# Attention followed by a mixture of experts: the order of vector work around seven-product matrix multiplications, scalar work in program order, and the last stores on two queues

## The chip, the cores and the metric

The kernel runs on one core of one Trainium2 chip. The metric is the device time of one execution in microseconds (us). Engines are named as in the profile: PE multiplies matrices (PEld is its weight load), DVE is the vector engine, ACT the scalar engine, POOL is GpSimd, SP only issues transfers. PE leaves its results in *banks* of a memory called PSUM, where DVE and ACT read them.

## The reference

Attention of 4 batches, 8 heads, 768 positions and head size 64 gives x of 3072 tokens by 512. Routing weights P come from x by eight rounds of row and column normalization. Then each of 8 experts is applied to every token:

```python
for e in range(E):                       # 8 experts
    h = np.maximum(x @ w1[e], 0.0)       # 3072 x 1024
    ye = h @ w2[e]                       # 3072 x 512
    out += P[:, e:e + 1] * ye
```

## The kernel before

Expert 0 is computed inside the attention stage. Experts 1 to 7 run in 42 *steps*, one for each expert e and chunk c of 512 tokens. Both layers of a step use seven half-size products in place of eight (the Strassen scheme), on sums and differences that DVE makes beforehand: S of the left factor, T of the right. Layer 1 does its seven products twice, for two halves g of the hidden units. A pair (g, k) below is product k of half g. Layer 2 of a step runs interleaved with layer 1 of the following step, in seven slots:

```python
        def step(g, k):
            ...                                    # cut
            if k == 6:
                product(g, 6, "y"); copy("2", "y")       # ACT: R copy of PSUM bank y
            if k == 7:
                product(g, 7, "y"); relu_sum(g, 1, 1, "y", "5")   # DVE reads bank y
            if k == 3:
                product(g, 3, "w", last=True); relu_sum(g, 0, 1, "w", "2")
            if k == 4:
                product(g, 4, "y", last=True)            # PE adds into bank y again
                nc.scalar.activation(out=block(g, 1, 0), in_=banks["y"], func=AF.Relu, ...)
        for pair in (((0, 1), (0, 2)), ((0, 6), (0, 5)), ((0, 7), (0, 3)), ((0, 4), (1, 1)),
                     ((1, 6), (1, 5)), ((1, 7), (1, 2)), ((1, 3), (1, 4))):
            for g, k in pair: step(g, k)
            yield
```

```python
    with tc.manual_schedule(engines={mybir.EngineType.DVE}):     # DVE runs in program order
        ...                                                      # cut
            if e == 1:
                weight_first(c)               # ACT: acc *= P[:, 0], all four blocks at once
                xg = combine_x((c + 1) % NCH)
            for slot in range(7):
                run(l1g, 1); run(l2g, 1)      # (shortened)
                if slot == 0: run(hg, 1)      # S of layer 2: second of four
                if slot == 1: run(hg, 2)      # third and fourth
                if slot in (3, 4):
                    run(wg, 1)                # weight combination for the next expert
                    run(xg, 2)                # T of x, only in the first expert
            hg = combine_h(e, c); run(hg, 1)  # first of four S
```

Only DVE runs in program order. A scheduler orders PE and ACT when the program is built, from its own estimates. Layer 2's products are added into acc with their routing weight: four of seven by DVE, three by ACT into an `add` buffer and from there by an accumulating transfer. In the last step DVE does all seven. The stores of the last expert go out through SP.

A reader of the timelines needs a few names. `acc` is the running sum of the output. `R` is ACT's copy of a bank whose sum isn't finished; a *relu sum* of DVE adds such a copy to a bank and cuts off below 0. `l1y<-T,w` is product 4 of layer 1, alone in having T and w as inputs. `hT<-l1y` on DVE is the relu sum of product 7, which reads the same bank. `S<-hT` is a combination for layer 2, `S<-w` (or `T<-w`) one for the next expert's weights.

The softmax here doesn't subtract the row's maximum and nothing guards it: scores larger than these inputs give would overflow.

Of the kernel before, what the change touches and what calls it, by code (L numbers as in the profile page):

```python
# [10 lines left out]
F32 = mybir.dt.float32  # L11
F16 = mybir.dt.float16
U32 = mybir.dt.uint32
AF = mybir.ActivationFunctionType
# [25 lines left out]
def kernel(  # L40
# [13 lines left out]
    nc = tc.nc  # L54
# [3 lines left out]
    E = moe_w_gate.shape[1]  # L58
# [93 lines left out]
    def load_expert(e):  # L152
        return load_w1(e), load_w2(e)

    expw = {}
# [212 lines left out]
    def run(g, n):  # L368
        for _ in range(n):
            if next(g, "end") == "end":  # L370
                return False
        return True
# [164 lines left out]
    def weight_first(c):  # L537

        for nb in range(4 * c, 4 * c + 4):
            nc.scalar.activation(out=acc_of(nb), in_=acc_of(nb), func=AF.Copy,  # L540
                                 bias=0.0, scale=Pne[:, nb, 0:1])

    works = [(e, c) for e in range(1, E) for c in range(NCH)]
    lefts1, rights1, lefts2, rights2, hTs = {}, {}, {}, {}, {}
# [45 lines left out]
    def layer1_plain(e, c):  # L590
        new_h(e, c)
        w1 = expw[e][0]
        for fb in range(8):
            l1 = psB.tile([128, CH], F32, tag="l1", name="l1b")
            for dc in range(4):
                nc.tensor.matmul(
                    out=l1, lhsT=w1[:, dc, ts(fb, 128)], rhs=xT[dc // 2][:, dc % 2, ts(c, CH)],
                    start=(dc == 0), stop=(dc == 3),
                )
            nc.scalar.activation(out=hTs[e, c][:, :, fb, :],  # L600
                                 in_=l1.rearrange("p (q m) -> p q m", q=2), func=AF.Relu,
                                 bias=0.0, scale=1.0)
            yield

    def layer1(e, c):

        new_h(e, c)
        h = hTs[e, c]
        banks, R = {}, {}

        def product(g, k, bank, first=False, last=False):
            if first:
                banks[bank] = psB.tile([128, 2, 256], F32, tag="l1", name=f"l1{bank}")
            for f in range(2):
                for dc in range(2):
                    nc.tensor.matmul(  # L616
                        out=banks[bank][:, f, :],
                        lhsT=lefts1[e][k - 1][:, dc, ts(2 * g + f, 128)],
                        rhs=rights1[c][k - 1][:, dc, :], start=(first and f == 0 and dc == 0),
                        stop=(last and f == 1 and dc == 1), skip_group_check=True,  # L620
                    )

        def copy(name, bank):
            R[name] = mp.tile([128, 2, 256], F32, tag=f"R{name}", bufs=1, name=f"R{name}")
            nc.scalar.activation(out=R[name], in_=banks[bank], func=AF.Copy, bias=0.0, scale=1.0)  # L625

        def block(g, i, n):
            return h[:, n, 4 * i + 2 * g:4 * i + 2 * g + 2, :]

        def relu_sum(g, i, n, bank, name):  # L630
            nc.vector._custom_dve(TENSOR_ADD_SAT, out=block(g, i, n), in0=banks[bank],  # L631
                                  in1=R[name], s0=65504.0, s1=0.0)

        def step(g, k):
            if k == 1:
                product(g, 1, "y", first=True)
                copy("1", "y")
            if k == 2:
                product(g, 2, "z", first=True, last=True)
                relu_sum(g, 0, 0, "z", "1")  # L640
            if k == 6:
                product(g, 6, "y")
                copy("2", "y")
            if k == 5:
                product(g, 5, "w", first=True)
                copy("5", "w")
            if k == 7:
                product(g, 7, "y")
                relu_sum(g, 1, 1, "y", "5")
            if k == 3:  # L650
                product(g, 3, "w", last=True)
                relu_sum(g, 0, 1, "w", "2")
            if k == 4:
                product(g, 4, "y", last=True)
                nc.scalar.activation(out=block(g, 1, 0), in_=banks["y"], func=AF.Relu,  # L655
                                     bias=0.0, scale=1.0)

        for pair in (((0, 1), (0, 2)), ((0, 6), (0, 5)), ((0, 7), (0, 3)), ((0, 4), (1, 1)),
                     ((1, 6), (1, 5)), ((1, 7), (1, 2)), ((1, 3), (1, 4))):
            for g, k in pair:  # L660
                step(g, k)
            yield

    def store(c, i, n):
        for o in range(2):
            nc.sync.dma_start(
                out=out[ts(c, CH), :].rearrange("(q i p c) (n d) -> i n c p q d", q=2, i=2, c=2, n=2)[i, n, o],
                in_=acc[c][64 * o:64 * o + 64, i, n, :, :],
            )

    def layer2(e, c):
        banks = {}
        final = (e, c) == works[-1]

        def product(k, bank, first, last=False):
            if first:
                banks[bank] = psB.tile([128, 2, 256], F32, tag="l2", name=f"l2{bank}")
            for q in range(2):
                for f in range(4):
                    nc.tensor.matmul(  # L680
                        out=banks[bank][:, q, :], lhsT=lefts2[e, c][k - 1][:, q, f, :],
                        rhs=rights2[e][k - 1][:, f, :], start=(first and q == 0 and f == 0),
                        stop=(last and q == 1 and f == 3), skip_group_check=True,
                    )

        def add(bank, i, n, by_dma):
            if by_dma:
                t = mp.tile([128, 2, 256], F32, tag="add", bufs=3, name="add")
            for q in range(2):
                dst = acc[c][:, i, n, q, :]  # L690
                w = Pne[:, 4 * c + 2 * q + i, e:e + 1]
                if by_dma:
                    nc.scalar.activation(out=t[:, q, :], in_=banks[bank][:, q, :], func=AF.Copy,  # L693
                                         bias=0.0, scale=w)
                else:
                    nc.vector.scalar_tensor_tensor(  # L696
                        out=dst, in0=banks[bank][:, q, :], scalar=w, in1=dst,
                        op0=ALU.mult, op1=ALU.add,
                    )
            if by_dma:  # L700
                nc.gpsimd.dma_start(out=acc[c][:, i, n, :, :], in_=t, accum_op=ALU.add)  # L701


        steps = {
            1: ("y", True, False, (0, 0)), 2: ("z", True, True, (0, 0)), 5: ("w", True, False, (1, 1)),
            6: ("y", False, False, (0, 1)), 3: ("w", False, True, (0, 1)),
            7: ("y", False, False, (1, 1)), 4: ("y", False, True, (1, 0)),
        }
        done = {}
        for k in (1, 5, 6, 2, 7, 3, 4):  # L710
            bank, first, last, (i, n) = steps[k]
            product(k, bank, first, last)
            add(bank, i, n, k in (2, 3, 4) and not final)
            done[i, n] = done.get((i, n), 0) + 1
            if e == E - 1 and done[i, n] == (1 if (i, n) == (1, 0) else 2):
                store(c, i, n)
            yield



    with tc.manual_schedule(engines={mybir.EngineType.DVE}):
        l1g, l2g, hg, wg, xg = layer1_plain(*works[0]), iter(()), iter(()), iter(()), iter(())
        for n, (e, c) in enumerate(works):
            if c == 0 and e + 1 < E:
                expw[e + 1] = load_expert(e + 1)
            if c == 2 and e + 1 < E:
                wg = combine_w(e + 1)
            if e == 1:
                weight_first(c)
                xg = combine_x((c + 1) % NCH)  # L730
            for slot in range(7):
                run(l1g, 2 if n == 0 and slot == 0 else 1)
                run(l2g, 1)
                if slot == 0:
                    run(hg, 1)
                if slot == 1:
                    run(hg, 2)
                if n == 0:
                    if slot == 0:
                        run(combine_w(1), 9)  # L740
                if slot in (3, 4):
                    run(wg, 1)
                    run(xg, 2)
            hg = combine_h(e, c)
            run(hg, 1)
            l2g = layer2(e, c)
            if n + 1 < len(works):
                l1g = layer1(*works[n + 1])
        run(hg, 9)
        run(l2g, 9)  # L750


# [33 lines left out]
```

## Time and profile before

The kernel takes 745.61 us (median of 15 runs; 744.29 to 746.96). I split the profiled execution by instructions:

| stretch | from, to (us) | length |
|---|---|---|
| attention and routing | 0 to the first matmul of expert 1, 206.66 | 206.66 |
| expert 1, up to the seventh start of layer 2 | 206.66 to 292.08 | 85.41 |
| 34 steady steps | 292.08 to 717.36 | 425.28 |
| last step's layer 1 | 717.36 to 728.91 | 11.55 |
| tail: last layer 2, stores, end | 728.91 to 745.55 | 16.64 |

(The starts used are those of layer 2's first product, `l2y<-w,hT`.) The busy times on the page, and the window view for the steady stretch (window, its length, busy us and instructions of each engine, granted clock, DMA busy share, GB/s):

```profile
PE 718.8 (96%) x7078; PEld 582.5 (78%) x7078; DVE 564.7 (76%) x1115; ACT 426.7 (57%) x794; POOL 156.5 (21%) x190
...
292.08:717.36 425.28, 424.00 (x3811) 372.19 (x3808) 347.85 (x652) 229.19 (x477) 92.47 (x110) 1.00 0.56 94
```

PE looks full: 424.00 of 425.28 us. That is misleading, because a matmul's slice (0.27 us) is longer than the distance between two starts (0.109 us), so short holes are covered. The Trainium skill says so too ("Perfetto Trace Analysis", "Identifying the Most-Contended Engine": matmul busy time is no measure of the distance to the limit, the weight loads' share is better). Here weight loads fill 372.19/425.28 = 87.5%; one takes 97.7 ns on the mean, so dense issue would give 97.7/109.1 = 89.6%. The two holes are in the timeline (start, duration, engine, line, operation, tiles, shapes, count, and in brackets the idle time before with its releaser). A light step, which makes no weight combination:

```profile
508.62 0.68 DVE L553 TENSOR_TENSOR S<-hT 128x1024 f16<-128x1024 f16 x1
...
509.21 0.68 DVE L553 TENSOR_TENSOR S<-hT,S 128x1024 f16<-128x1024 f16 x1
...
509.81 0.71 PE L680 MATMUL l2z<-w,hT 128*128 128x256 f16 x5
509.82 0.68 DVE L631 CUSTOM_DVE_ANT_0 hT<-l1y,R 128x512 f16<-128x512 f32 x1
...
510.55 0.60 PE L616 MATMUL l1y<-T,w 128*128 128x256 f16 x4
510.55 0.31 PEld L616 LDWEIGHTS <-w 128*128 128x128 f16 x3 [0.21 <-issue]
```

Five l2z matmuls from 509.81 would let the next start at 510.36, but product 4 starts at 510.55. The profile calls the wait "issue", that is, it shows no cause; the neighbour on DVE does: the relu sum that reads the bank ends at 509.82 + 0.68 = 510.50. DVE did it late because two S, from 508.62 on, came first. A heavy step (four of six chunks) has a second hole, before product (1,4):

```profile
312.76 0.88 DVE L696 SCALAR_TENSOR_TENSOR acc<-l2y,Pne,acc 128x256 f32<-128x256 f32 x2 [0.78 <-PE l2y L680]
...
313.56 0.68 DVE L553 TENSOR_TENSOR S<-S,w 128x1024 f16<-128x1024 f16 x1
314.15 0.68 DVE L631 CUSTOM_DVE_ANT_0 hT<-l1y,R 128x512 f16<-128x512 f32 x1
314.31 0.60 PE L616 MATMUL l1w<-xT,S 128*128 128x256 f16 x4
...
314.89 0.60 PE L616 MATMUL l1y<-T,w 128*128 128x256 f16 x4
```

DVE idles 0.78 us for an accumulation's product and then does a weight combination ahead of the relu sum, which ends at 314.83. Product (1,4) could start at 314.75, 0.44 after `l1w`, and starts at 314.89. Light steps take 12.42 us and heavy ones 12.57, where 112 matmuls of 109.1 ns make 12.22.

In expert 1, ACT weights all of acc in a crowd (the source view: count, durations, first and last start):

```profile
L540 ACT ACTIVATE acc<-acc,Pne x24: 705/779/867, 208.7 to 233.5; 128x512 f32<-128x512 f32 x24
```

At the end, the timeline shows SP's last stores and DVE's last accumulation, the window view how busy the DMA engines are meanwhile:

```profile
729.60 12.35 SPq L666 DMA_DIRECT2D out_dram<-acc  x15
737.40 0.88 DVE L696 SCALAR_TENSOR_TENSOR acc<-l2y,Pne,acc 128x256 f32<-128x256 f32 x2 [0.34 <-PE l2y L680]
...
738.00:743.00 5.00, 0.00 (x0) 0.00 (x0) 0.28 (x1) 0.00 (x0) 0.00 (x0) 0.76 0.93 196
```

DVE is done at 738.28, yet the program ends at 745.55. In the trace the last ten stores leave SP 0.67 us apart, from 735.29 to 741.34.

### The profile page before, as it was taken

What the parts mean: (1) busy time and instruction counts of PE and PEld (TensorE: products, weight loads), DVE (VectorE), ACT (ScalarE), POOL (GpSimd) and SP (SyncE); (2) the same over time, 40 slices, a digit from 0 to 9 for tenths busy, and PEclk for the clock granted to TensorE, in tenths of its full rate; (3) what the DMA queues carried; (4) which work ended last, traced back from release to release, by engine and by line L of the source; (5) the groups of instructions that cost most, each with busy time, mean ns of one, the idle gap of its engine ahead of it and who ended that gap; (6) DMA issues with size and microseconds to landing.
All of it is one profiled execution on the core that took longest, in us unless ns stands there. A gap on an engine that the chain in (4) does not pass through costs nothing.

```text
span 745.6 us, 17358 instructions
## 1 busy us (share of the span) xinstructions
PE 718.8 (96%) x7078; PEld 582.5 (78%) x7078; DVE 564.7 (76%) x1115; ACT 426.7 (57%) x794; POOL 156.5 (21%) x190
## 2 busy tenths in 40 slices
PE   6999999999999999999999999999999999999994
PEld 2566666766668888888888888888888888888883
DVE  6557465664778998788778878887888788877775
ACT  2766677767488454545555555555555555555551
POOL 8313021000002122212221131213121312121210
PEclk8899999999999999999999999999999999999998
DMA  9999475200063339543954396438643864245877
GB/s 123 187 172 84 47 58 46 29 2 2 4 110 68 62 58 147 94 72 57 145 98 71 58 141 102 72 58 132 109 72 55 136 105 77 48 81 104 153 146 152
DMA packets 84656, 65.89 MB, mean 88 GB/s; under 512 B 50400, under 2 KB 64736, under 8 KB 84576
## 3 DMA queue, kind: packets, MB, share of 16 engines
q0 software_dynamic: 77520, 58.48, 55.2%
q1 hardware_dynamic: 7056, 6.30, 3.7%
q8 instruction: 55, 0.90, 0.5%
q14 instruction: 25, 0.20, 0.1%
HBM read 52.45 MB, written 6.29 MB: 79 GB/s over the span
## 4 chain that ended last, share of the span: by engine, by line
PE 64%; DVE 3%; issue 1%; ACT 0%; DVEq 0%; ACTq 0%
PE l1y L616 19%; PE l2y L680 18%; PE l2w L680 9%; PE l1w L616 9%; PE l1z L616 5%; PE l2z L680 4%; DVE S L553 1%; DVE acc L696 1%; DVE hT L631 1%; ACT R L625 0%; ACT hT L655 0%; ACT add L693 0%; DVEq L781 0%; ACTq L625 0%; ACTq L693 0%
## 5 line engine op out<-in xcount | busy, mean ns | idle before, releaser
L701 POOL DMA_DIRECT2D acc<-add x123 | 103.5, 841 | 402.6 <-ACT add L693 377.0
L625 ACT ACTIVATE R<-l1y 128x512 f32<-128x512 f32 x164 | 98.9, 603 | 126.6 <-PE l1y L616 91.7
L680 PEld LDWEIGHTS <-S 128*128 128x128 f16 x1344 | 131.5, 98 | 16.3 <-issue 1.1
L616 PEld LDWEIGHTS <-S 128*128 128x128 f16 x1312 | 128.3, 98 | 17.2 <-issue 1.9
L696 DVE SCALAR_TENSOR_TENSOR acc<-l2y,Pne,acc 128x256 f32<-128x256 f32 x254 | 110.3, 475 | 39.3 <-PE l2y L680 39.3
L616 PEld LDWEIGHTS <-w 128*128 128x128 f16 x984 | 95.8, 97 | 23.0 <-issue 12.0
L680 PEld LDWEIGHTS <-hT 128*128 128x128 f16 x1008 | 98.5, 98 | 12.7 <-issue 1.1
L429 ACT ACTIVATE PT<-sc 128x1024 f16<-128x1024 f32 (+1 forms) x96 | 84.2, 919 | 40.5 <-PE sc L420 38.3
L616 PE MATMUL l1y<-T,S 128*128 128x256 f16 x656 | 98.4, 272 | 0.9 <-ACT R L625 0.7
L680 PE MATMUL l2y<-T,S 128*128 128x256 f16 x672 | 87.1, 273 | 0.7 <-DVE acc L696 0.6
L631 DVE CUSTOM_DVE_ANT_0 hT<-l1z,R 128x512 f16<-128x512 f32 x82 | 56.2, 685 | 35.8 <-ACT R L625 35.2
L693 ACT ACTIVATE add<-l2w,Pne 128x256 f32<-128x256 f32 x82 | 34.5, 472 | 61.0 <-PE l2w L680 59.4
L655 ACT ACTIVATE hT<-l1y 128x512 f16<-128x512 f32 x82 | 49.1, 599 | 30.5 <-PE l1y L616 30.0
L553 DVE TENSOR_TENSOR S<-hT 128x1024 f16<-128x1024 f16 x84 | 57.6, 686 | 11.7 <-ACT hT L655 6.7
L631 DVE CUSTOM_DVE_ANT_0 hT<-l1w,R 128x512 f16<-128x512 f32 x82 | 55.8, 681 | 1.8
L631 DVE CUSTOM_DVE_ANT_0 hT<-l1y,R 128x512 f16<-128x512 f32 x82 | 55.8, 681 | 0.0
L616 PE MATMUL l1y<-T,w 128*128 128x256 f16 x328 | 49.0, 271 | 1.5
L680 PE MATMUL l2z<-w,hT 128*128 128x256 f16 x336 | 50.2, 273 | 0.0
L625 ACT ACTIVATE R<-l1w 128x512 f32<-128x512 f32 x82 | 49.8, 608 | 0.0
L341 PE MATMUL l<-xT,w 128*128 128x256 f16 x384 | 47.9, 273 | 1.8 <-ACT hT L346 0.7
L616 PE MATMUL l1w<-T,S 128*128 128x256 f16 x328 | 49.4, 273 | 0.0
L616 PE MATMUL l1y<-xT,w 128*128 128x256 f16 x328 | 49.4, 273 | 0.0
(102 smaller groups left out, 1121.0 us busy)
## 6 DMA issues: line engine op xcount, KB each, us to landing
acc<-add POOLq DMA_DIRECT2D x123, 256.0 KB, 3.3
w<-in_moe_w_dram POOLq DMA_DIRECT2D x16, 1024.0 KB, 10.4
out_dram<-acc SPq DMA_DIRECT2D x48, 128.0 KB, 2.7
k<-in_k_dram POOLq DMA_DIRECT2D x11, 256.0 KB, 4.7
q<-in_q_dram POOLq DMA_DIRECT2D x11, 256.0 KB, 6.8
v<-in_v_dram POOLq DMA_DIRECT2D x12, 192.0 KB, 7.7
acc<-in_v_dram POOLq DMA_DIRECT2D x3, 256.0 KB, 7.8
k<-in_k_dram POOLq DMA_DIRECT2D x2, 128.0 KB, 3.5
```

Source lines behind the costliest of these rows:

```text
L341: nc.tensor.matmul(out=l1[:, ts(fb % 2, 256)], lhsT=w1[:, dc, ts(fb, 128)], rhs=xT[dc // 2][:, dc % 2, c0:c0 + 256], start=(dc == 0), stop ...
L429: nc.scalar.activation(out=PT[:, :, c0:c0 + width], in_=sc[:, :, 0:width], func=AF.Exp, bias=0.0, scale=SCALE,)
L553: nc.vector.tensor_tensor(out=out_, in0=a_, in1=b_, op=op)
L616: nc.tensor.matmul(out=banks[bank][:, f, :], lhsT=lefts1[e][k - 1][:, dc, ts(2 * g + f, 128)], rhs=rights1[c][k - 1][:, dc, :], start=(fir ...
L625: nc.scalar.activation(out=R[name], in_=banks[bank], func=AF.Copy, bias=0.0, scale=1.0)
L631: nc.vector._custom_dve(TENSOR_ADD_SAT, out=block(g, i, n), in0=banks[bank], in1=R[name], s0=65504.0, s1=0.0)
L655: nc.scalar.activation(out=block(g, 1, 0), in_=banks["y"], func=AF.Relu, bias=0.0, scale=1.0)
L680: nc.tensor.matmul(out=banks[bank][:, q, :], lhsT=lefts2[e, c][k - 1][:, q, f, :], rhs=rights2[e][k - 1][:, f, :], start=(first and q == 0 ...
L693: nc.scalar.activation(out=t[:, q, :], in_=banks[bank][:, q, :], func=AF.Copy, bias=0.0, scale=w)
L696: nc.vector.scalar_tensor_tensor(out=dst, in0=banks[bank][:, q, :], scalar=w, in1=dst, op0=ALU.mult, op1=ALU.add,)
L701: nc.gpsimd.dma_start(out=acc[c][:, i, n, :, :], in_=t, accum_op=ALU.add)
```

## The change

Its intent: DVE should reach the relu sums before PE needs their banks, ACT should weight acc little by little, and the tail should overlap better. The core of the diff:

```diff
             nc.scalar.activation(out=acc_of(nb), in_=acc_of(nb), func=AF.Copy,
                                  bias=0.0, scale=Pne[:, nb, 0:1])
+            yield
 ...  (banks keyed by [g, bank] instead of [bank])
-        for pair in (..., ((0, 7), (0, 3)), ((0, 4), (1, 1)),
+        for pair in (..., ((0, 7), (0, 3)), ((1, 1), (0, 4)),
 ...
-            nc.sync.dma_start(
+            (nc.scalar if c == NCH - 1 and (i == n or (n and o)) else nc.sync).dma_start(
 ...  (layer 2, last step only: each half q of a product in a PSUM bank of its own)
+            if first and final:
+                banks[bank] = [psB.tile([128, 512], F32, tag="l1" if bank == "y" else "l2",
+                                        name=f"l2{bank}{q}")[:, 0:256] for q in range(2)]
 ...
-                t = mp.tile([128, 2, 256], F32, tag="add", bufs=3, name="add")
+                t = mp.tile([128, 2, 256], F32, tag="add", bufs=5, name="add")
 ...  (main loop)
+            if slot in (2, 4):
+                go("first", 2)        # two weightings of acc
-                if slot == 0: run(hg, 1)
-                if slot == 1: run(hg, 2)
+            if slot in (0, 2, 3):
+                go("h")
-                if slot in (3, 4): run(wg, 1)
+            if slot == 3:
+                go("w", 2)
 ...
+    with tc.manual_schedule(engines={DVE, ACT}):      # from step 1 on: ACT in program order too
```

More of the change, by code (lines that the diff above doesn't have):

```diff
@@ L612, in product @@
             if first:
-                banks[bank] = psB.tile([128, 2, 256], F32, tag="l1", name=f"l1{bank}")
+                banks[g, bank] = psB.tile([128, 2, 256], F32, tag="l1", name=f"l1{bank}")
             for f in range(2):
@@ L616, in product @@
                     nc.tensor.matmul(
-                        out=banks[bank][:, f, :],
+                        out=banks[g, bank][:, f, :],
                         lhsT=lefts1[e][k - 1][:, dc, ts(2 * g + f, 128)],
@@ L621, in product, with copy @@
                     )
-        def copy(name, bank):
+        def copy(g, name, bank):
             R[name] = mp.tile([128, 2, 256], F32, tag=f"R{name}", bufs=1, name=f"R{name}")
-            nc.scalar.activation(out=R[name], in_=banks[bank], func=AF.Copy, bias=0.0, scale=1.0)
+            nc.scalar.activation(out=R[name], in_=banks[g, bank], func=AF.Copy, bias=0.0, scale=1.0)
         def block(g, i, n):
@@ L630, in relu_sum @@
         def relu_sum(g, i, n, bank, name):
-            nc.vector._custom_dve(TENSOR_ADD_SAT, out=block(g, i, n), in0=banks[bank],
+            nc.vector._custom_dve(TENSOR_ADD_SAT, out=block(g, i, n), in0=banks[g, bank],
                                   in1=R[name], s0=65504.0, s1=0.0)
@@ L636, in step @@
                 product(g, 1, "y", first=True)
-                copy("1", "y")
+                copy(g, "1", "y")
             if k == 2:
@@ L642, in step @@
                 product(g, 6, "y")
-                copy("2", "y")
+                copy(g, "2", "y")
             if k == 5:
                 product(g, 5, "w", first=True)
-                copy("5", "w")
+                copy(g, "5", "w")
             if k == 7:
@@ L654, in step @@
                 product(g, 4, "y", last=True)
-                nc.scalar.activation(out=block(g, 1, 0), in_=banks["y"], func=AF.Relu,
+                nc.scalar.activation(out=block(g, 1, 0), in_=banks[g, "y"], func=AF.Relu,
                                      bias=0.0, scale=1.0)
-        for pair in (((0, 1), (0, 2)), ((0, 6), (0, 5)), ((0, 7), (0, 3)), ((0, 4), (1, 1)),
+        for pair in (((0, 1), (0, 2)), ((0, 6), (0, 5)), ((0, 7), (0, 3)), ((1, 1), (0, 4)),
                      ((1, 6), (1, 5)), ((1, 7), (1, 2)), ((1, 3), (1, 4))):
@@ L675, in product @@
         def product(k, bank, first, last=False):
-            if first:
-                banks[bank] = psB.tile([128, 2, 256], F32, tag="l2", name=f"l2{bank}")
+            if first and final:
+                banks[bank] = [psB.tile([128, 512], F32, tag="l1" if bank == "y" else "l2",
+                                        name=f"l2{bank}{q}")[:, 0:256] for q in range(2)]
+            elif first:
+                t = psB.tile([128, 2, 256], F32, tag="l2", name=f"l2{bank}")
+                banks[bank] = [t[:, q, :] for q in range(2)]
             for q in range(2):
@@ L680, in product @@
                     nc.tensor.matmul(
-                        out=banks[bank][:, q, :], lhsT=lefts2[e, c][k - 1][:, q, f, :],
-                        rhs=rights2[e][k - 1][:, f, :], start=(first and q == 0 and f == 0),
-                        stop=(last and q == 1 and f == 3), skip_group_check=True,
+                        out=banks[bank][q], lhsT=lefts2[e, c][k - 1][:, q, f, :],
+                        rhs=rights2[e][k - 1][:, f, :],
+                        start=(first and (final or q == 0) and f == 0),
+                        stop=(last and (final or q == 1) and f == 3), skip_group_check=True,
                     )
@@ L692, in add @@
                 if by_dma:
-                    nc.scalar.activation(out=t[:, q, :], in_=banks[bank][:, q, :], func=AF.Copy,
+                    nc.scalar.activation(out=t[:, q, :], in_=banks[bank][q], func=AF.Copy,
                                          bias=0.0, scale=w)
@@ L696, in add @@
                     nc.vector.scalar_tensor_tensor(
-                        out=dst, in0=banks[bank][:, q, :], scalar=w, in1=dst,
+                        out=dst, in0=banks[bank][q], scalar=w, in1=dst,
                         op0=ALU.mult, op1=ALU.add,
@@ L717, in layer2 @@
             yield
-    with tc.manual_schedule(engines={mybir.EngineType.DVE}):
-        l1g, l2g, hg, wg, xg = layer1_plain(*works[0]), iter(()), iter(()), iter(()), iter(())
-        for n, (e, c) in enumerate(works):
-            if c == 0 and e + 1 < E:
-                expw[e + 1] = load_expert(e + 1)
-            if c == 2 and e + 1 < E:
-                wg = combine_w(e + 1)
-            if e == 1:
-                weight_first(c)
-                xg = combine_x((c + 1) % NCH)
-            for slot in range(7):
-                run(l1g, 2 if n == 0 and slot == 0 else 1)
-                run(l2g, 1)
-                if slot == 0:
-                    run(hg, 1)
-                if slot == 1:
-                    run(hg, 2)
-                if n == 0:
-                    if slot == 0:
-                        run(combine_w(1), 9)
-                if slot in (3, 4):
-                    run(wg, 1)
-                    run(xg, 2)
-            hg = combine_h(e, c)
-            run(hg, 1)
-            l2g = layer2(e, c)
-            if n + 1 < len(works):
-                l1g = layer1(*works[n + 1])
-        run(hg, 9)
-        run(l2g, 9)
+    gens = {name: iter(()) for name in ("l1", "l2", "h", "w", "x", "first")}
@@ new lines, with go, body @@
+    gens["l1"] = layer1_plain(*works[0])
+    def go(name, n=1):
+        run(gens[name], n)
+    def body(n):
+        e, c = works[n]
+        if c == 0 and e + 1 < E:
+            expw[e + 1] = load_expert(e + 1)
+        if c == 2 and e + 1 < E:
+            gens["w"] = combine_w(e + 1)
+        if e == 1:
+            gens["first"] = weight_first(c)
+            gens["x"] = combine_x((c + 1) % NCH)
+        for slot in range(7):
+            go("l1", 2 if n == 0 and slot == 0 else 1)
+            go("l2")
+            if slot in (2, 4):
+                go("first", 2)
+            if slot in (0, 2, 3):
+                go("h")
+            if n == 0 and slot == 0:
+                run(combine_w(1), 9)
+            if slot == 3:
+                go("w", 2)
+            if slot in (3, 4):
+                go("x", 2)
+        gens["h"] = combine_h(e, c)
+        go("h")
+        gens["l2"] = layer2(e, c)
+        if n + 1 < len(works):
+            gens["l1"] = layer1(*works[n + 1])
@@ L754 @@
+    DVE, ACT = mybir.EngineType.DVE, mybir.EngineType.Activation
+    with tc.manual_schedule(engines={DVE}):
+        body(0)
+    with tc.manual_schedule(engines={DVE, ACT}):
+        for n in range(1, len(works)):
+            body(n)
+        for _ in range(7):
+            go("h")
+            go("l2")
 _INS = ['q', 'k', 'v', 'is_retrieval', 'n_sink', 'window', 'moe_w_gate', 'moe_w1', 'moe_w2']
```

## The prediction

> **What bounds it.** PE is busy 96% (the page), and 424.0 of 425.3 us from 292.1 to 717.4 (window view). But busy is not dense: starts of 128x256 matmuls lie 109.1 ns apart (timeline), as 256/2.4 GHz + 2.5 ns = 109.2 says (the Trainium skill, "TensorE: Matmul & The Clock Gate", "Wait — 56ns, not 53.3ns?"). One step (expert, chunk) has 112 matmuls: 12.22 us if dense. The timeline shows 12.42 us (chunks without weight combinations) and 12.57 (the four with them). The extra: 0.20 us before product (0,4), which waits until the DVE relu sum has read the same bank (510.50 us; PE goes on at 510.55), because DVE does two combinations S first; and 0.15 us before (1,4) in heavy chunks.
>
> **The change, part by part**
>
> 1. DVE does relu sums (0,7), (0,3) and one accumulation before the last two S. Laid out with traced issue spacings (S 0.60, relu 0.60, accumulation 0.39 us), relu (0,7) ends at 509.3; PE needs it at 509.8 ((0,4) moves ahead of l2z). The S are ready at 511.3 and 511.9, needed at 512.0 and 513.7. For (1,4): ready 514.5, needed 515.05, also after two weight combinations. Both stalls go: 12.22 us per step. 34 pitches, 425.3 us, become 415.5: -9.8 us.
> 2. First expert (207 to 292 us). Weighting acc is spread out instead of filling ACT (15.0 of 15 us busy in 215 to 230); PE's holes at 211.8, 217.6 and 229.8 go. But chunks with x and w combinations are bound by DVE (about 12.0 us of work plus 0.6 of waits, 12.70 pitch); that work stays: about 12.65. I get -2.6 us by 292 us.
> 3. Tail (728.9 us to end). Before: PE and DVE alternate on one bank, DVE ends at 738.3; ten stores leave SP 0.65 us apart (735.3 to 741.3), the last lands at 743.7. Halves in separate banks let PE write one while DVE reads the other; DVE ends about 1.5 us earlier. ACT takes five stores. But the DMA engines are 0.9 busy then, and the skill's front page ("Trainium Kernel Development and Optimization", "Key Constraints") says that queues share them and a second issuer saves only issue time. The hole around 736 us (DMA 0.2 to 0.4) is filled. I count -2.2 us (last step included).
> 4. More add buffers: one DMA wait of 1.6 us in all, off the chain; 0. Attention (to 206.7 us) is unchanged in the built order.
>
> Sum -14.6 us; I take off 0.4 for new in-order waits on ACT (order in steady steps nearly as before).
>
> **Predicted: 731.4 us**, 728.5 to 736.0 eight times in ten. Chances: over 2% faster 0.42, within 2% 0.57, slower 0.01. The 2% line (730.7) lies almost at my centre.
>
> **What would show it.** PE pitch 12.2 in experts 2 to 7, no PE hole before (0,4) or (1,4); pitch 12.6 to 12.7 in the first expert's last chunks, PE waiting at (1,4); DVE's busy time unchanged; last accumulation to end of span about 6 us instead of 7.3; ACT's weighting spread to about 280 us.
>
> **What would make it wrong.** The ACT order making PE wait for R copies or l1 banks (margins 0.2 to 0.5 us); DVE late for (1,4) in heavy chunks (0.1 us per step is 3.6 us); DVE in the first expert slower than laid out (up to +2); stores bound by DMA bandwidth, so that the tail saves only 1, or spread better, so that it saves 3.5.

## The result

The changed kernel takes 731.60 us (median of 8 runs, 729.44 to 732.17). The ratio to the kernel before is 0.9805, with a 95% interval of 0.9793 to 0.9817. The interval lies on both sides of the 2% line. By stretches of the two profiles:

| stretch | before | after | saved | predicted |
|---|---|---|---|---|
| attention and routing | 206.66 | 203.99 | 2.67 | 0 |
| expert 1 | 85.41 | 83.07 | 2.34 | 2.6 |
| 34 steady steps | 425.28 | 415.71 | 9.57 | 9.8 |
| last layer 1 and tail | 28.19 | 25.54 | 2.65 | 2.2 |

The first row isn't the change's doing; it is explained under the experiments. The other three give 14.56 us, and the medians 14.0. The page and the window view of the steady stretch after:

```profile
PE 706.6 (97%) x7078; PEld 582.3 (80%) x7078; DVE 566.2 (78%) x1115; ACT 428.1 (59%) x794; POOL 156.4 (21%) x190
...
287.06:702.76 415.70, 415.70 (x3810) 372.61 (x3808) 349.59 (x652) 229.64 (x477) 92.51 (x110) 1.00 0.58 96
```

The work is the same (weight loads 372.61 us, DVE 349.59), and it is denser: weight loads now fill 89.6%, the dense value. All 34 steps take 12.23 us. The places of the two holes, first the light step, then a heavy one:

```profile
498.53 0.68 DVE L632 CUSTOM_DVE_ANT_0 hT<-l1y,R 128x512 f16<-128x512 f32 x1
...
499.28 0.60 PE L617 MATMUL l1y<-xT,w 128*128 128x256 f16 x4
499.71 0.60 PE L617 MATMUL l1y<-T,w 128*128 128x256 f16 x4
...
499.92 0.60 ACT L626 ACTIVATE R<-l1y 128x512 f32<-128x512 f32 x1 [2.36 <-PE l1y L617]
...
500.41 0.59 ACT L656 ACTIVATE hT<-l1y 128x512 f16<-128x512 f32 x1
500.50 0.68 DVE L554 TENSOR_TENSOR S<-hT 128x1024 f16<-128x1024 f16 x1
...
501.02 0.60 PE L617 MATMUL l1y<-T,S 128*128 128x256 f16 x4
```

```profile
306.80 0.69 DVE L554 TENSOR_TENSOR S<-S,w 128x1024 f16<-128x1024 f16 x1
...
308.19 0.68 DVE L632 CUSTOM_DVE_ANT_0 hT<-l1y,R 128x512 f16<-128x512 f32 x1
...
308.89 0.60 PE L617 MATMUL l1w<-xT,S 128*128 128x256 f16 x4
309.33 0.60 PE L617 MATMUL l1y<-T,w 128*128 128x256 f16 x4
```

The relu sum ends at 499.21, half a microsecond ahead of product 4 at 499.71; before it ended after PE wanted to go on. In the heavy step it ends at 308.87, ahead of 309.33. The last lines of the light step will matter below: ACT does the R copy (499.92) ahead of the relu of (0,4) (500.41), and product (1,6) follows at 501.02 without a hole. The weighting in expert 1, and the end:

```profile
L540 ACT ACTIVATE acc<-acc,Pne x24: 710/724/742, 206.0 to 270.8; 128x512 f32<-128x512 f32 x24
...
719.86 4.12 ACTq L667 DMA_DIRECT2D out_dram<-acc  x5
...
721.32 0.86 DVE L703 SCALAR_TENSOR_TENSOR acc<-l2y,Pne,acc 128x256 f32<-128x256 f32 x2
...
722.00:726.00 4.00, 0.00 (x0) 0.00 (x0) 0.18 (x1) 0.00 (x0) 0.00 (x0) 0.88 0.98 257
```

The weighting now stretches over 65 us. DVE's last accumulation ends at 722.18, 6.13 us before the end (728.31) instead of 7.27. The DMA engines are 0.98 busy instead of 0.93, and move 257 GB/s instead of 196: that pair of numbers returns below.

### The profile page after: what moved, and what is told of

Read it like the earlier page. It is cut to its first block, busy times and chain, and to the rows that moved or that the text cites. A ratio compares the mean times of both kernels' runs of the same rounds, so it can differ in the third digit from the quotient of the medians.

```text
span 728.3 us, 17354 instructions
## 1 busy us (share of the span) xinstructions
PE 706.6 (97%) x7078; PEld 582.3 (80%) x7078; DVE 566.2 (78%) x1115; ACT 428.1 (59%) x794; POOL 156.4 (21%) x190
## 4 chain that ended last, share of the span: by engine, by line
PE 81%; DVE 9%; ACT 5%; issue 2%; POOL 1%; DMA 1%; DVEq 0%; POOLq 0%; ACTq 0%
PE l1y L617 18%; PE l2y L686 18%; PE l2w L686 9%; PE l1w L617 9%; PE l1z L617 5%; PE l L355 5%; PE l2z L686 4%; PE l L341 4%; ACT PT L429 3%; PE sc L420 2%; PE pv L298 2%; PE pv L291 2%; DVE acc L703 2%; DVE S L554 1%; DVE hT L632 1%
## 5 line engine op out<-in xcount | busy, mean ns | idle before, releaser
L617 PE MATMUL l1z<-xT,w 128*128 128x256 f16 x328 | 49.2, 273 | 0.0
```

Source lines behind the costliest of these rows:

```text
L617: nc.tensor.matmul(out=banks[g, bank][:, f, :], lhsT=lefts1[e][k - 1][:, dc, ts(2 * g + f, 128)], rhs=rights1[c][k - 1][:, dc, :], start=( ...
```

## The experiments

The theories before the runs. A: the steady gain is DVE's order alone; expert 1 gains by ACT's order and is then held by DVE; in the tail the issue of stores is what counts. B, in several forms: ACT's order makes the steady holes; bandwidth of the DMA engines, or the end of DVE's work, holds the tail. Eleven runs told them apart. Stretches are measured as in the tables above; the sum from the first matmul of expert 1 to the end is 538.89 us before and 524.32 after.

| run | median us (runs) | ratio, 95% interval | expert 1 | 34 steps | tail |
|---|---|---|---|---|---|
| h_only | 738.66 (4) | 0.9905, 0.9887 to 0.9923 | 85.24 | 419.68 | 16.64 |
| w_only | 743.24 (4) | 0.9965, 0.9947 to 0.9982 | 85.14 | 423.52 | 16.28 |
| h_and_w | 736.80 (4) | 0.9883, 0.9863 to 0.9902 | 85.11 | 416.79 | 16.46 |
| no_swap | 731.89 (4) | 0.9824, 0.9808 to 0.9839 | 83.15 | 416.79 | 14.25 |
| act_free | 732.69 (4) | 0.9825, 0.9812 to 0.9839 | 84.86 | 415.71 | 14.25 |
| all_sp | 733.77 (4) | 0.9842, 0.9820 to 0.9863 | 83.08 | 415.71 | 16.92 |
| one_bank | 731.52 (4) | 0.9804, 0.9785 to 0.9823 | 83.09 | 415.71 | 14.15 |
| bufs3 | 731.48 (4) | 0.9812, 0.9796 to 0.9829 | 83.08 | 415.71 | 14.15 |
| after_again | 730.88 (6) | 0.9795, 0.9782 to 0.9808 | 83.05 | 415.71 | 14.30 |
| dve_level | 729.61 (4) | 0.9785, 0.9772 to 0.9799 | 81.44 | 415.71 | 14.24 |
| dve_level_pool | 729.14 (4) | 0.9780, 0.9765 to 0.9796 | 81.44 | 415.71 | 14.04 |

All gave correct results. Effects of 1 us are smaller than the spread of single executions, so the verdicts below rest on the stretches, which repeat to about 0.1 us.

### DVE's order, one edit at a time

h_only is the kernel before with the S moved:

```diff
-                if slot == 0:
-                    run(hg, 1)
-                if slot == 1:
-                    run(hg, 2)
+                if slot in (0, 2, 3):
+                    run(hg, 1)
```

> The kernel before with one edit: the combinations S of layer 2 are emitted in slots 0, 2 and 3 instead of 0, 1 and 1, so that DVE reaches the relu sum of product 7 before the last two S. Theory A (the hole before product (0,4) is PE waiting for that relu sum, and DVE's order alone makes it): the steady pitch goes from 12.42 to 12.22 us in light steps and from 12.57 to about 12.35 in heavy ones (S now fill some of DVE's idle time before the accumulation of product 7), some 7 us in all. Rival B (the order on ACT, which this edit leaves to the scheduler, makes the holes): pitches stay at 12.42 and 12.57 and the time within 1 us. First expert and tail: unchanged under both.

The steady stretch fell by 5.60 us, where some 7 had been expected: light steps to 12.26, heavy ones to 12.40. The hole before (0,4) is gone with ACT's order left to the scheduler, so rival B falls for it. What I hadn't expected is a rest of 0.035 us in every step. The timeline shows it before product (1,6):

```profile
455.25 0.60 ACT L655 ACTIVATE hT<-l1y 128x512 f16<-128x512 f32 x1 [2.36 <-PE l1y L616]
...
455.49 1.04 PE L680 MATMUL l2z<-w,hT 128*128 128x256 f16 x8
455.75 0.60 ACT L625 ACTIVATE R<-l1y 128x512 f32<-128x512 f32 x1
...
456.40 0.60 PE L616 MATMUL l1y<-T,S 128*128 128x256 f16 x4
```

Eight l2z matmuls end their issue at 455.49 + 0.87 = 456.36. ACT's R copy, done after the relu of (0,4), ends at 456.35, and PE adds into the copied bank from 456.40. PE goes on 0.05 us after the end of the instruction it waited for, as it did before product (0,4) (510.50 and 510.55).

w_only moves both weight combinations of a step into the idle time:

```diff
-                if slot in (3, 4):
-                    run(wg, 1)
-                    run(xg, 2)
+                if slot == 3:
+                    run(wg, 2)
+                if slot in (3, 4):
+                    run(xg, 2)
```

> The kernel before with one edit: both weight combinations of a heavy step are emitted in slot 3 instead of one each in slots 3 and 4. Theory A: the second hole of heavy steps, 0.15 us before product (1,4), comes from DVE idling for the accumulation of product 7 and then doing a weight combination ahead of the relu sum; with both combinations in that idle time the hole goes and heavy steps take 12.42 us as light ones do, while the 0.20 us before (0,4) stays: some 3 us in all. Rival B (ACT's order): nothing changes. A third possibility, that DVE has too much work in heavy steps whatever the order: heavy steps stay at 12.57.

32 of 34 steps took 12.43 us: the heavy steps' second hole is gone, with the same amount of work on DVE. The stretch fell by 1.76 us only, because one step took 13.38:

```profile
514.74 0.84 ACT L693 ACTIVATE add<-l2y,Pne 128x256 f32<-128x256 f32 x2 [1.39 <-DMA acc<-add]
...
516.12 0.60 PE L616 MATMUL l1y<-T,S 128*128 128x256 f16 x4 [0.78 <-ACT R L625]
```

All three add buffers were still being read by accumulating transfers, ACT stood still for 1.39 us, and PE waited for the R copy behind it. This happened while the next expert's weights were loaded.

h_and_w has both edits.

> The kernel before with both edits of DVE's order (S in slots 0, 2, 3; both weight combinations in slot 3), nothing else. Theory A (DVE's order makes both steady holes): no hole before (0,4) or (1,4); what stays is the 0.035 us a step seen with the S edit alone before product (1,6), so 12.26 us in light and heavy steps, 34 of them 416.8 us, some 8.4 us less than before. If the two edits interfere, heavy steps stay near 12.4.

All 34 steps took 12.26 us, 416.79 in all: 8.49 us of the steady gain is DVE's order, and the edits add up (5.60, and 2.71 without the one step of 13.38, make 8.31).

### The exchanged pair, and ACT's order

Exchanging (0,4) and (1,1) in the kernel before, with the banks keyed by half as the exchange needs and nothing else, gives a built program whose order on PE, DVE and ACT is the same as before instruction by instruction (only buffer names differ), because the scheduler orders PE and ACT by its own estimates. It was not run. So the exchange was undone in the changed kernel instead (no_swap):

```diff
-((0, 7), (0, 3)), ((1, 1), (0, 4)),
+((0, 7), (0, 3)), ((0, 4), (1, 1)),
```

> The changed kernel with the pair of products in the old order again, (0,4) ahead of (1,1), DVE and ACT in program order. Theory A (the 0.035 us before product (1,6) is PE waiting for the R copy of (1,1), which ACT does after the relu of (0,4) when that comes first in the program): 12.26 us per steady step, 34 steps 1.2 us longer than in the changed kernel, hole before (1,6) only. Rival B (it belongs to the scheduler's ACT order): 12.23, no hole.

Again 12.26 us in all 34 steps, and the only hole is the one before (1,6). With DVE's order in place, the exchange is worth 416.79 - 415.71 = 1.08 us in the steady stretch: ACT then does the R copy of (1,1) ahead of the relu of (0,4). ACT's program order has no part in it: without either of the two the stretch takes 416.79 us (h_and_w), with ACT's order alone 416.79 (no_swap), with the exchange alone 415.71 (act_free, next), with both 415.71.

act_free leaves ACT's order to the scheduler in the changed kernel:

```diff
-    with tc.manual_schedule(engines={DVE, ACT}):
+    with tc.manual_schedule(engines={DVE}):
```

> The changed kernel with ACT's order left to the scheduler again (only DVE in program order). Its built order crowds the weighting of acc into the first steps again, as before the change. Theory A (crowding makes PE's holes at the start of the first expert): the first expert is 1.0 to 1.6 us longer than in the changed kernel, the 34 steady steps stay at 12.23. Rival B (ACT's program order is what made the steady steps dense): steady steps rise above 12.3.

Expert 1 took 84.86 us, 1.79 more than in the changed kernel (1.0 to 1.6 had been expected), with the steady steps unchanged. The source view of this run dates the weighting of acc from 206.2 to 231.1 us, crowded as before, although the code yields after each. It is ACT's program order that spreads it. Four times before 228 us, PE waits for an R copy in this run, with 0.43 to 0.62 us lost each time; the changed kernel has no such hole. The last of the four, where the copy stands behind a weighting and an accumulation:

```profile
225.23 0.83 ACT L540 ACTIVATE acc<-acc,Pne 128x512 f32<-128x512 f32 x1
225.85 0.95 ACT L700 ACTIVATE add<-l2y,Pne 128x256 f32<-128x256 f32 x2
...
226.56 0.73 ACT L626 ACTIVATE R<-l1y 128x512 f32<-128x512 f32 x1
...
227.34 0.60 PE L617 MATMUL l1y<-T,S 128*128 128x256 f16 x4 [0.46 <-ACT R L626]
```

(In the steady steps, the scheduler, given the exchanged pair and DVE's new order, also found the good order for the R copy.)

### DVE in the first expert

Four steps of expert 1 stay at 12.63 to 12.73 us after the change. dve_level starts the weight combinations of expert 2 one step earlier, one per step, and moves half of the x combinations behind the first S of the next step, where DVE idled for an R copy:

```diff
-        if c == 2 and e + 1 < E:
+        if c == (1 if e == 1 else 2) and e + 1 < E:
             gens["w"] = combine_w(e + 1)
 ...
             if slot == 3:
-                go("w", 2)
-            if slot in (3, 4):
+                go("w", 1 if e == 1 else 2)
                 go("x", 2)
         gens["h"] = combine_h(e, c)
         go("h")
+        go("x", 2)
```

> The changed kernel with the first expert's DVE work levelled: the weight combinations of expert 2 start one step earlier, one per step instead of two, and the second half of the x combinations moves behind the first S of the next step, where DVE idled 0.6 to 0.8 us for an R copy. Theory A (the four steps of 12.63 to 12.73 us in the first expert are DVE having about 12 us of work plus fixed waits): each falls to 12.2 to 12.3 us, the first expert is 1.6 to 2.0 us shorter, the whole near 729.8. Rival B (those steps are long because ACT now carries two weightings of acc between its copies): no gain.

All four steps fell to 12.23 us, though ACT carries the same weightings; the step before them rose from 12.33 to 12.53. The two edits weren't tried apart. The timelines of the changed kernel and of this run, at product (1,4) in the same step:

```profile
247.09 0.68 DVE L632 CUSTOM_DVE_ANT_0 hT<-l1y,R 128x512 f16<-128x512 f32 x1
...
247.82 0.60 PE L617 MATMUL l1y<-T,w 128*128 128x256 f16 x4 [0.25 <-DVE hT L632]
```

```profile
247.21 0.68 DVE L632 CUSTOM_DVE_ANT_0 hT<-l1y,R 128x512 f16<-128x512 f32 x1
...
247.84 0.60 PE L617 MATMUL l1w<-xT,S 128*128 128x256 f16 x4
...
248.28 0.60 PE L617 MATMUL l1y<-T,w 128*128 128x256 f16 x4
```

In the first, PE starts as soon as the relu sum ends (247.77); in the second the sum is done at 247.89, 0.39 us early. From the first matmul of expert 1 to the end this kernel takes 522.74 us, where the changed kernel took 524.32 and 524.42. By this stretch it beats both kernels. By single executions (729.61 against 730.88 us on the same chip) the intervals still overlap; the 1.6 us rest on the stretch.

after_again is the changed kernel, as partner on the same chip.

> The changed kernel once more, as the partner of the next two runs on the same chip: again near 731.6 us. The stretches from the first matmul of expert 1 on should repeat the first profile to within 0.1 us (83.1 us to the seventh step, 34 steps of 12.23, 14.2 us after the last step's layer 1 products), while the start before it may differ by a few us from run to run, since the two first profiles differed by 2.7 us within the first 25 us of the same code.

It repeated all stretches to 0.11 us, but its profile reached expert 1 at 207.70 us, where the first one did at 203.99.

### Start-up noise

The code up to expert 1 is the same in all 13 profiles, and they reach it between 203.46 and 207.70 us. The time from PE's 161st matmul, at 24 to 28 us, to expert 1 is 179.37 to 179.42 us in all of them. So the difference arises in the first 28 us. It goes with the half-speed clock at the start: the trace's clock record shows it for 6.83 us in seven profiles (arrival 203.5 to 205.1), for 10.24 in five (205.4 to 206.7) and for 13.65 in one (207.7). The Trainium skill ("TensorE: Matmul & The Clock Gate", "What's actually happening") describes a free-running window of 3413 ns; these lengths are two, three and four such windows, so the lengths agree, and whether the window runs freely isn't shown. The end of the half-speed stretch, between 17.6 and 25.0 us, tells more than its length: a straight line through the 13 profiles gives 0.50 us of later arrival for each us of a later end, and misses none by more than 0.62 us. Why a run gets two, three or four windows was not tested.

### The tail

all_sp is the changed kernel with all stores on SP:

```diff
-            (nc.scalar if c == NCH - 1 and (i == n or (n and o)) else nc.sync).dma_start(
+            nc.sync.dma_start(
```

> The changed kernel, but with the last chunk's five stores moved back from ACT to SP. Theory A (SP's issue, 0.65 us a store, paces the tail, not the bandwidth of the DMA engines): the ten last stores leave SP 0.65 us apart from about 16.5 us after the start of the last step's layer 1 products, the last lands about 2 us later than in the changed kernel. Rival B (the prediction's: the DMA engines are nearly full, a second issuer saves only issue time that overlaps): at most 0.5 us later.

DVE's last accumulation kept its place (8.06 us into the tail), but the tail grew from 14.19 to 16.92 us, longer than before the change. The source view of the stores (ns: shortest, median, longest issue), and the window view during the last stores of this run:

```profile
L667 SPq DMA_DIRECT2D out_dram<-acc x48: 595/598/1562, 663.6 to 727.5; - x48
...
724.00:729.00 5.00, 0.00 (x0) 0.00 (x0) 0.00 (x0) 0.00 (x0) 0.00 (x0) 0.75 0.92 194
```

With one issuer the engines show 0.92 busy at 194 GB/s; with two, 0.98 at 257. The ten last landings are 0.68 us apart in this run and 0.51 in the changed kernel. One issue holds SP for 0.60 us, and the last ten follow each other 0.67 us apart, so SP issues nearly without a pause. A packet takes 69 ns on the mean in the one window and 55 in the other: its recorded time was longer where fewer stores were in flight. The busy share is a sum of such times, and it can even pass 1 (1.09 in w_only from 510 to 513 us). So a busy share of 0.92 did not mean that the engines were full: SP's issue paced them. Rival B falls. Of the 2.73 us, 2.24 lie before the last landing; the other 0.49 come after it, where the program ends 1.83 us later with one issuer and 1.34 with two, for a reason that wasn't tested.

one_bank puts the two halves of a product into one bank again in the last step:

```diff
-            if first and final:
+            if first and False:
 ...
-    start=(first and (final or q == 0) and f == 0), stop=(last and (final or q == 1) and f == 3)
+    start=(first and q == 0 and f == 0), stop=(last and q == 1 and f == 3)
```

> The changed kernel, but in the last step the two halves of a product share one PSUM bank again. Theory A: DVE and PE take turns on the bank and DVE's last accumulation ends 1.0 to 1.5 us later; as the last store of the changed kernel leaves late for another reason (at 724.2 us, 2 us after the last accumulation, when an earlier store lands at 724.20), the end comes only 0.2 to 0.5 us later. Rival B (the last accumulation paces the end): the end comes as much later as the last accumulation, 1.0 to 1.5 us.

```profile
721.94 0.88 DVE L703 SCALAR_TENSOR_TENSOR acc<-l2y,Pne,acc 128x256 f32<-128x256 f32 x2 [0.45 <-PE l2y L686]
...
723.94 0.88 DVE L703 SCALAR_TENSOR_TENSOR acc<-l2y,Pne,acc 128x256 f32<-128x256 f32 x2 [0.34 <-PE l2y L686]
```

PE and DVE take turns again and DVE ends 0.98 us later (9.04 against 8.06 us into the tail), yet the tail is 14.15 us, not longer at all (0.2 to 0.5 us had been expected). The Trainium skill ("PSUM — Partial Sum Buffer", "PSUM bank collisions raise a hardware error") says why the program must take turns: two engines may not touch one bank in the same partitions at once, and the hardware does not arbitrate. The waits above are the program's own; no run here provoked the error. The separate banks do what they were made for, and it is worth nothing here, because the last store leaves as late (10.1 us into the tail in both kernels) and the stores finish as late.

dve_level_pool gives GpSimd two of the last chunk's stores, on top of dve_level, and moves one more from SP to ACT:

```diff
-            (nc.scalar if c == NCH - 1 and (i == n or (n and o)) else nc.sync).dma_start(
+            last = c == NCH - 1
+            (nc.gpsimd if last and i == n == 0 else
+             nc.scalar if last and (i == n or o) else nc.sync).dma_start(
```

> As the run before, and the last chunk's first two stores (block 0,0) are issued by GpSimd, with the others split between ACT and SP. Theory A: the end is paced by the issue of the last stores, of which the very last waits for the landing of an earlier store (issued at 724.21 us in the changed kernel, with a landing at 724.20); with two stores on another kind of queue, the last store waits for one that landed earlier, leaves about 1 us sooner and the end comes 0.7 to 1.3 us sooner. Rival B (bandwidth of the DMA engines paces the end): within 0.3 us.

The last store left 0.86 us sooner in the tail (9.28 us into it, against 10.15 in dve_level), but the last landing came at 13.07 us instead of 12.90; the end came at 14.04 instead of 14.24 only because it followed the last landing by 0.97 us instead of 1.33. So the late last store was not what held the end, and my theory A falls here: once two queues issue, a third gains nothing that one profile can show. What then holds the last landing, the DMA engines themselves or something else, no run isolates.

### Three add buffers

bufs3 undoes the five buffers in the changed kernel:

```diff
-                t = mp.tile([128, 2, 256], F32, tag="add", bufs=5, name="add")
+                t = mp.tile([128, 2, 256], F32, tag="add", bufs=3, name="add")
```

> The changed kernel with three add buffers again instead of five. The prediction counted them as worth 0. Theory A: ACT waits once to three times in a run for an accumulating transfer (1.4 to 2.2 us each, as in the kernel before and in the two runs of single DVE edits) when the next expert's weights are being loaded; once in a while such a wait reaches PE, as one did with 0.95 us in the run of the weight edit: 0 to 2 us longer, steady pitch 12.23 but for a few steps. Rival B (never on PE's path): all 34 steps 12.23.

All 34 steps took 12.23 us, and its waits list no wait of ACT for an accumulating transfer. The profiles of the kernel before, of the two single edits and of h_and_w list one to three, of 1.4 to 2.3 us each. So in this profile three buffers cost nothing, and theory A's waits did not come. Why they occur in the earlier orders and not in this one stays open; one profile can't exclude a rare one.

## Why the prediction was right

731.4 us was predicted, 731.60 measured, and the range held. The 2% line was put almost at the centre, and the interval of the ratio indeed contains 0.98. That the total came so near is in part luck: the first two terms were 0.23 and 0.26 us too large, the tail's gain was 0.45 too small, and the 0.4 us taken off for ACT did not come.

1. *Steady steps, -9.8 us.* Measured -9.57. Both named holes existed and went, by DVE's order as argued: h_only and w_only each remove one, and h_and_w gives 8.49 us. The margins came out as laid out from the trace's issue spacings (0.5 us ahead of (0,4)). The argument had left out one thing: with DVE's order alone 0.035 us a step stay, and it takes the exchanged pair, which the prediction used for another purpose, to remove the last 1.08 us.
2. *First expert, -2.6 us.* Measured -2.34. The holes from crowded weighting went: 1.79 us by ACT's order. The four steps held by DVE were predicted at about 12.65 us and took 12.63 to 12.73; dve_level shows that DVE was indeed what held them.
3. *Tail, -2.2 us with the last step.* Measured -2.65. The size was near by luck, for the reason was wrong. The prediction credited the earlier end of DVE and the filled DMA hole, and held the second issuer to be worth little because the DMA engines were 0.9 busy. The runs show the reverse: without the second issuer the whole tail gain is lost (all_sp), without the separate banks nothing is (one_bank).
4. *Buffers, 0.* In the changed kernel they are worth nothing that one profile shows. In w_only such a wait reached PE once and cost 0.95 us, so "off the chain" was true of the profile read, not of the earlier order in general.
5. *ACT in program order, +0.4 us.* The cost did not come: the order saves 1.79 us in the first expert and neither costs nor saves in the steady steps (act_free).

The profile's signs came nearly as listed: 12.23 us steps without holes, PE waiting at (1,4) in expert 1, weighting until 271 us (about 280 was predicted), 6.13 us from the last accumulation to the end.

## What to carry to other kernels

When the busiest engine shows 99.7% busy, compare the distance between its starts with the dense one: here 2.3% of the steady time hid in holes of 0.15 to 0.20 us, and they came from another engine doing independent work ahead of the read that frees a bank. Put such work where that engine idles anyway, and check by the built order whether an edit moves anything at all. Test a queue's second issuer instead of ruling it out by a high DMA busy share, and compare kernels from an instruction after the start-up when effects of 1 us matter.

## What the Trainium skill lacked or had wrong

- "DMA: Bandwidth & Descriptors", section "Issuing engines are not separate DMA queues", says that a second issuer saves only the issue time, which is usually small relative to the transfer. For these 128 KB stores of 1 KB rows it was not small: landings 0.68 us apart with one issuer, 0.51 with two, and 2.7 us of the tail. This is a point on that section alone.
- No page puts a number on how high the busy share of the DMA engines can be while stores wait for their issuer: 0.92 to 0.93 at 194 to 196 GB/s with one issuer, 0.98 at 257 GB/s with two; mean packet times of 69 and 55 ns.
- "TensorE: Matmul & The Clock Gate" calls the start-up ramp small (under 1% of a typical kernel) and variable between runs, and this agrees: half speed lasts 6.83, 10.24 or 13.65 us, and the arrival at expert 1 moves with its end by up to 4.2 us, 0.6% of the time. That is still more than most of the effects measured here, and no page advises to compare two profiles of one kernel from an instruction after the ramp.
- No page says that a wait of PEld without a listed cause ("issue" in these profiles) can be a wait for another engine's read of a bank: 0.21 us before product (0,4), 0.05 us after the end of the DVE instruction that reads it, and gone when that instruction was moved forward (h_only).
